# One scheduled graph of small tasks, with DMA transposes from block 3 on, for chunk-selected attention and a softplus MLP

## The chip, the cores and the metric

The kernel runs on one core of a Trainium2 chip. A core has a matmul engine (TensorE, PE in the profile), a vector engine (VectorE, DVE), an activation engine (ScalarE, ACT), a general engine (GpSimd, POOL) and a queue engine (SyncE, SP). Each works through its own program in order; they meet at semaphores. Sixteen DMA engines move data. SBUF is the on-chip memory, PSUM the eight banks into which TensorE writes. The metric is the device time of one execution in microseconds (us).

## What is computed

```python
def _attn_ref(q, k, v):                      # (4, 8, 768, 64) each
    k_min, k_max = np.min(k_chunks, axis=3), np.max(k_chunks, axis=3)   # chunks of 32 keys
    ub = np.sum(np.maximum(q * k_min, q * k_max), axis=-1)              # a bound per query and chunk
    ub = np.where(causal, ub, -1000000000.0)
    top_chunks = np.argsort(ub, axis=-1)[..., -top_k:]                  # top_k = 6 of 24 chunks
    scores = scale * np.matmul(q, k.transpose(0, 1, 3, 2))
    mask = sel & (pos[:, None] >= pos[None, :])                         # chosen chunks, causal
    attn = softmax(np.where(mask, scores, -1000000000.0))
    return np.matmul(attn, v)

def _moe_ref(x, w_in, w_out):                # x (3072, 512), w_in (512, 2048), w_out (2048, 512)
    h = x @ w_in
    g = np.maximum(h, 0.0) + np.log1p(np.exp(-np.abs(h)))               # softplus
    return g @ w_out
```

The heads of the attention output side by side (8 x 64 = 512) are the MLP's input. Inputs and outputs are float32; the kernel computes in bfloat16 with float32 sums.

## The kernel before

The work is cut into 12 blocks: 4 batches by 3 blocks of 256 queries. A block goes through three stages.

The preparation (`prep_block`, L163) transposes k and q on TensorE by the identity matrix (L175, L191) so that the head dimension lies on partitions, two heads a tile; `kT` goes to SBUF on ScalarE (L179), and VectorE takes maximum and minimum of each chunk (L181, L182). Positive and negative parts of q (L203, L204) times these give the bounds `ub` (L212, L213, 48 columns each). VectorE adds the causal mask, finds the eight largest (L224), and writes which chunks lie below the sixth (`mraw`, L226). This is transposed too (`mT`, L236) and put beside q into `qa` and `qt`, so that the score matmul itself, with one-hot rows `ohb` in `KA` and `KB`, pushes chunks that were not chosen far down.

The attention goes by head pair `p` and head `h`: scores (L263, L265), the exponential on ScalarE into `pt` (L267), the causal mask of the diagonal on GpSimd (L271), then `o_ps` from `pt` and v (L285), one over the sum (L291), the product (L293), a transpose (L304) and a copy into the MLP's input `x` (L305).

The MLP: `hp` from `w_in_sb` and `x` (L322), exponential (L324) and logarithm of one plus it (L326) on ScalarE, which is the softplus, then `y` from `g` and `w_out_sb` (L335), a copy (L340) and a store of 128 rows.

The order is written out by hand. `run_block` walks the score steps of one block; after each, `slot` advances one waiting step of `later` (L285 and on), some steps of `mlp_stream` by a rate, whatever `agenda` has for this slot (the preparation of the next block, in five pieces) and one load. The lines that set it:

```python
        credit[0] += rate
        while credit[0] >= 1.0:
            credit[0] -= 1.0
            if next(mlp, "end") == "wait":
                credit[0] = 0.0
        for g_ in agenda.pop(clock[0], []):
            next(g_, None)
        if loads and next(loads[0], "end") == "end":
            loads.popleft()
```

Blocks 0 to 2 are loaded as float32 from SyncE and ScalarE (L90) and cast on ScalarE (L103); the others are loaded and cast by DMAs issued on GpSimd (L108, L114), as are the weights (L149, L155). Four DMAs from SyncE fill the one-hot rows (L142, L143). PSUM is split into fixed pools: two banks for scores, one for `o_ps`, two for transposes and bounds, two for `hp`, one for `y`.

Of the kernel before, what the change touches and what calls it, by code (L numbers as in the profile page):

```python
# [15 lines left out]
ET = mybir.EngineType  # L16


@with_exitstack
def kernel(  # L20
# [10 lines left out]
    B, H, S, D = q.shape  # L31
    CH = 32
    NCH = S // CH
    TOPK = 6
    NQT = S // 128
    NP = H // 2
    scale = 1.0 / math.sqrt(D)
    NEG = -30000.0 / scale

    d_model, d_ff = moe_w_in.shape  # L40
    KDM = d_model // 128
    KFF = d_ff // 128
    QB = 256
    NT = QB // 128
    NBLK = S // QB
    NCB = QB // CH
    blocks = [(b, blk) for b in range(B) for blk in range(NBLK)]
    NB = len(blocks)

    ctx.enter_context(tc.manual_schedule(engines={ET.Pool, ET.SP}))  # L50
    nc.scalar.preload_act_table_set("natural_log_exp_and_others")

    PS = bass.MemoryType.PSUM
    singles = ctx.enter_context(tc.tile_pool(name="singles", bufs=1))
    f_pool = ctx.enter_context(tc.tile_pool(name="f", bufs=6))
    io_pool = ctx.enter_context(tc.tile_pool(name="io", bufs=3))
    qt_pool = ctx.enter_context(tc.tile_pool(name="qt", bufs=3))
    prep = ctx.enter_context(tc.tile_pool(name="prep", bufs=2))
    pt_pool = ctx.enter_context(tc.tile_pool(name="pt", bufs=3))
    st_pool = ctx.enter_context(tc.tile_pool(name="st", bufs=3))  # L60
    x_pool = ctx.enter_context(tc.tile_pool(name="x", bufs=4))
    g_pool = ctx.enter_context(tc.tile_pool(name="g", bufs=3))
    e_pool = ctx.enter_context(tc.tile_pool(name="e", bufs=3))
    mo_pool = ctx.enter_context(tc.tile_pool(name="mo", bufs=3))
    ps_s = ctx.enter_context(tc.tile_pool(name="ps_s", bufs=2, space=PS))
    ps_o = ctx.enter_context(tc.tile_pool(name="ps_o", bufs=1, space=PS))
    ps_t = ctx.enter_context(tc.tile_pool(name="ps_t", bufs=2, space=PS))
    ps_h = ctx.enter_context(tc.tile_pool(name="ps_h", bufs=2, space=PS))
    ps_y = ctx.enter_context(tc.tile_pool(name="ps_y", bufs=1, space=PS))

    V = [singles.tile([128, NQT, H, D + 1], BF16, name=f"v_{i}") for i in range(2)]
    KA = [singles.tile([128, NP, S], BF16, name=f"ka_{i}") for i in range(2)]
    KB = [singles.tile([128, NP, S], BF16, name=f"kb_{i}") for i in range(2)]
    BD = [singles.tile([128, NP, 2, 2, NCH], BF16, name=f"bd_{i}") for i in range(2)]
    Mraw = [singles.tile([128, NP, NT, 2, 32], BF16, name=f"mraw_{i}") for i in range(2)]
    w_in_sb = singles.tile([128, KDM, d_ff], BF16, name="w_in_sb")
    w_out_sb = singles.tile([128, KFF, d_model], BF16, name="w_out_sb")

    src = {"k": k, "q": q, "v": v}
    xfs, loaded = {}, {}  # L80

    def rows(nm, n, t):
        b, blk = blocks[n]
        r0 = blk * QB + t * 128
        return src[nm][b, :, r0:r0 + 128].rearrange("h s d -> s h d")

    def load_f32(nm, n, eng):
        xf = f_pool.tile([128, NT, H, D], F32, name="xf")
        for t in range(NT):
            eng[t].dma_start(out=xf[:, t], in_=rows(nm, n, t))  # L90
        xfs[nm, n] = xf

    def v_dst(n, t):
        b, blk = blocks[n]
        return V[b % 2][:, blk * NT + t, :, 0:D]

    def cast_f32(nm, n):
        xf = xfs.pop((nm, n))
        if nm != "v":
            loaded[nm, n] = io_pool.tile([128, NT, H, D], BF16, name=nm + "_sb")  # L100
        for t in range(NT):
            dst = v_dst(n, t) if nm == "v" else loaded[nm, n][:, t]
            nc.scalar.copy(dst, xf[:, t])  # L103

    def load_cast(nm, n):
        if nm == "v":
            for t in range(NT):
                nc.gpsimd.dma_start(out=v_dst(n, t), in_=rows(nm, n, t))  # L108
                yield
        else:  # L110
            xb = io_pool.tile([128, NT, H, D], BF16, name=nm + "_sb")
            loaded[nm, n] = xb
            for t in range(NT):
                nc.gpsimd.dma_start(out=xb[:, t], in_=rows(nm, n, t))  # L114
                yield

    for nm in "kqv":
        load_f32(nm, 0, (nc.sync, nc.scalar))

    ident = singles.tile([128, 128], BF16)  # L120
    make_identity(nc, ident)
    ohb = singles.tile([32, S], BF16, name="ohb")
    nc.vector.memset(ohb, NEG)
    cmask = singles.tile([128, NQT, NCH], F32, name="cmask")
    nc.vector.memset(cmask, 0.0)
    nc.gpsimd.affine_select(out=ohb, in_=ohb, compare_op=ALU.is_ge, fill=0.0,
                            base=0, channel_multiplier=-CH, pattern=[[1, S]])
    nc.gpsimd.affine_select(out=ohb, in_=ohb, compare_op=ALU.is_ge, fill=0.0,
                            base=CH - 1, channel_multiplier=CH, pattern=[[-1, S]])
    nc.gpsimd.affine_select(out=ohb, in_=ohb, compare_op=ALU.not_equal, fill=-1.0,  # L130
                            base=-NCH, channel_multiplier=1, pattern=[[0, S]])
    nc.gpsimd.affine_select(out=cmask, in_=cmask, compare_op=ALU.is_ge, fill=-1.0e30,
                            base=0, channel_multiplier=1, pattern=[[128, NQT], [-CH, NCH]])

    for i in range(2):
        nc.vector.memset(Mraw[i], 0.0)

    def consts(i):
        nc.vector.memset(BD[i], 0.0)
        nc.vector.memset(KB[i][0:32], 0.0)  # L140
        nc.vector.memset(V[i][:, :, :, D:D + 1], 1.0)
        nc.sync.dma_start(out=KA[i][64:96], in_=ohb.unsqueeze(1).to_broadcast([32, NP, S]))  # L142
        nc.sync.dma_start(out=KB[i][32:64], in_=ohb.unsqueeze(1).to_broadcast([32, NP, S]))  # L143

    def load_w_in():
        for half in range(2):
            fs = slice(half * d_ff // 2, (half + 1) * d_ff // 2)
            for kt in range(KDM):
                nc.gpsimd.dma_start(out=w_in_sb[:, kt, fs],  # L149
                                    in_=moe_w_in[kt * 128:(kt + 1) * 128, fs])  # L150
                yield

    def load_w_out():
        for c4 in range(4):
            nc.gpsimd.dma_start(  # L155
                out=w_out_sb[:, c4 * 4:(c4 + 1) * 4, :],
                in_=moe_w_out[c4 * 512:(c4 + 1) * 512, :].rearrange(
                    "(kt ki) f -> ki kt f", ki=128))
            yield

    Q = {}

    def prep_block(n):  # L163
        b, blk = blocks[n]
# [81 lines left out]
        yield  # L246

    later = deque()
    clock = [0]
    X = {}  # L250

    def score_step(n, p):
# [234 lines left out]
```

The softmax here doesn't subtract the row's maximum and nothing guards it: scores larger than these inputs give would overflow.

## Time and profile before

| | |
|---|---|
| time, median of 2 runs | 316.94 us (316.83 to 317.06) |
| span of the profiled execution | 314.1 us |
| busy: PE, ACT, DVE, POOL | 270.5, 224.2, 174.4, 99.0 us |
| chain that ended last, by engine | PE 57%, DVE 26%, ACT 12% |
| PE matmuls of L322, L335 (busy) | 103.5, 90.7 us |
| score exponentials (L267), MLP exponentials (L324), logarithms (L326) | 103.9, 58.4, 51.8 us |
| DMA engines' share of q0 (issued on GpSimd) | 43.9% of the span |

The profile is of one execution. A group of instructions is given by its line, its engine, the tiles written and read and a count; behind the bar stand its busy time and the mean of one. Matmuls are pipelined: their durations overlap, and the gap between two starts says more than a duration. A timeline row is the start, the time covered, and what ran; "x8" means that eight equal instructions are merged; brackets hold the idle time before it and what ended that. In the row by slices each digit is the busy share of a fortieth of the span, in tenths.

### The profile page before, as it was taken

How to read it: one execution, taken by the hardware profiler on the slowest of the kernel's cores; microseconds unless marked ns; L12 is line 12 of the kernel's file. 1: busy time of each engine (PE TensorE's matmuls, PEld its weight loads, DVE VectorE, ACT ScalarE, POOL GpSimd, SP SyncE). 2: the span in 40 equal slices, each digit the busy share in tenths (PEclk: the TensorE clock that was granted, in tenths of full speed). 3: DMA queues.
4: the chain of work that ended last, by engine and by line, in shares of the span. 5: the costliest groups of instructions: out<-in, count | busy, mean ns of one | idle time of the engine just before them, and what ended most of it. 6: DMA issues, size and time to landing. Idle time of an engine off the chain costs nothing.

```text
span 314.1 us, 6878 instructions
## 1 busy us (share of the span) xinstructions
PE 270.5 (86%) x2748; PEld 198.6 (63%) x2784; DVE 174.4 (56%) x550; ACT 224.2 (71%) x379; POOL 99.0 (32%) x172
## 2 busy tenths in 40 slices
PE   1335879989899799899999799899999999999983
PEld 0223657667658667677658577677568777776651
DVE  5818582592965964935946946836748732112100
ACT  4578789968837858788628868888539769983550
POOL 4024375622723613514624414424421211111000
PEclk9999959999999999999999999999999999999999
DMA  9999899993933906904913905907900000001101
GB/s 165 200 216 216 147 158 189 92 71 45 80 73 52 83 11 60 101 2 57 90 59 53 83 35 33 102 3 76 94 33 35 3 33 35 2 33 35 67 17 52
DMA packets 82208, 23.51 MB, mean 75 GB/s; under 512 B 75520, under 2 KB 78080, under 8 KB 82176
## 3 DMA queue, kind: packets, MB, share of 16 engines
q0 software_dynamic: 59424, 11.28, 43.9%
q1 hardware_dynamic: 19632, 11.01, 14.3%
q10 hardware_dynamic: 3120, 0.79, 1.4%
q8 instruction: 21, 0.34, 0.4%
q14 instruction: 11, 0.09, 0.1%
HBM read 27.26 MB, written 6.29 MB: 107 GB/s over the span
## 4 chain that ended last, share of the span: by engine, by line
PE 57%; DVE 26%; ACT 12%; issue 2%; DMA 1%; ACTq 0%; DVEq 0%
PE y L335 21%; PE hp L322 17%; PE o_ps L285 5%; PE s_ps L263 4%; DVE kx L181 4%; ACT kt L179 4%; DVE kx L182 4%; PE s_ps L265 3%; PE mT L236 3%; ACT pt L267 2%; DVE qneg L204 2%; ACT e_sb L324 2%; DVE qpos L203 2%; DVE qt L200 2%; DMA xf<-in_k_dram 1%
## 5 line engine op out<-in xcount | busy, mean ns | idle before, releaser
L267 ACT ACTIVATE pt<-s_ps 128x512 bf16<-128x512 f32 (+1 forms) x192 | 103.9, 556 | 36.7 <-PE s_ps L265 29.9
L322 PE MATMUL hp<-x,w_in_sb 128*128 128x256 bf16 x768 | 103.5, 273 | 3.2 <-ACT e_sb L324 1.8
L271 POOL TENSOR_SCALAR_AFFINE_SELECT pt<-pt 128x256 bf16<-128x256 bf16 x96 | 40.9, 426 | 185.5 <-ACT pt L267 185.1
L335 PE MATMUL y<-w_out_sb,g 128*128 128x512 bf16 x348 | 90.7, 379 | 3.6 <-DVE y_sb L340 1.7
L322 PEld LDWEIGHTS <-w_in_sb 128*128 128x128 bf16 x768 | 71.4, 98 | 12.9 <-issue 4.1
L324 ACT ACTIVATE e_sb<-hp 128x512 f32<-128x512 f32 x96 | 58.4, 611 | 27.7 <-PE hp L322 27.4
L335 PEld LDWEIGHTS <-g 128*128 128x128 bf16 x384 | 34.2, 97 | 28.6 <-issue 2.8
L326 ACT ACTIVATE g<-e_sb 128x1024 bf16<-128x1024 f32 x48 | 51.8, 1078 | 0.3
L285 PEld LDWEIGHTS <-pt 128*128 128x128 bf16 x672 | 32.9, 99 | 11.1 <-issue 4.3
L340 DVE COPY y_sb<-y 128x512 f32<-128x512 f32 x24 | 16.5, 687 | 39.7 <-PE y L335 39.5
L291 DVE RECIPROCAL rec<-o_ps 128x4 f32<-128x4 f32 x48 | 8.5, 177 | 38.1 <-PE o_ps L285 37.9
L305 DVE COPY x<-oT 128x256 bf16<-128x256 bf16 x48 | 13.9, 289 | 25.1 <-PE oT L304 24.8
L285 PE MATMUL o_ps<-v_106,pt 128*128 128x65 bf16 x336 | 20.7, 199 | 2.2 <-DVE o_sb L293 1.9
L181 DVE TENSOR_REDUCE kx<-kt 128x32 bf16<-128x1024 bf16 x12 | 14.6, 1219 | 13.0 <-ACT kt L179 13.0
L293 DVE TENSOR_TENSOR o_sb<-o_ps,rec 128x256 bf16<-128x256 f32 x48 | 20.2, 422 | 1.3
L285 PE MATMUL o_ps<-v_107,pt 128*128 128x65 bf16 x336 | 18.4, 193 | 1.7 <-DVE o_sb L293 1.5
L304 PE MATMUL oT<-ident,o_sb 128*128 128x128 bf16 x96 | 13.7, 225 | 4.3 <-DVE o_sb L293 4.3
L114 POOL DMA_DIRECT2D k_sb<-in_k_dram x18 | 16.1, 892 | 0.8 <-issue 0.5
L114 POOL DMA_DIRECT2D q_sb<-in_q_dram x18 | 16.2, 902 | 0.4 <-issue 0.3
L175 PE MATMUL kT<-ident,k_sb 128*128 128x128 bf16 x96 | 8.8, 241 | 8.1 <-ACT k_sb L103 7.6
L263 PE MATMUL s_ps<-qt,kb_110 128*128 128x256 bf16 x48 | 14.0, 293 | 1.6 <-ACT pt L267 0.9
L263 PE MATMUL s_ps<-qa,ka_108 96*128 96x256 bf16 x48 | 14.2, 296 | 0.8 <-DVE qa L241 0.8
(111 smaller groups left out, 365.2 us busy)
## 6 DMA issues: line engine op xcount, KB each, us to landing
out_dram<-y_sb SPq DMA_DIRECT2D x24, 256.0 KB, 2.0
k_sb<-in_k_dram POOLq DMA_DIRECT2D x18, 128.0 KB, 3.8
q_sb<-in_q_dram POOLq DMA_DIRECT2D x18, 128.0 KB, 4.3
w_in_sb<-in_moe_w_in_dram POOLq DMA_DIRECT2D x8, 256.0 KB, 6.9
w_out_sb<-in_moe_w_out_dram POOLq DMA_DIRECT2D x4, 512.0 KB, 9.5
v_107<-in_v_dram POOLq DMA_DIRECT2D x12, 128.0 KB, 5.3
xf<-in_k_dram SPq DMA_DIRECT2D x5, 256.0 KB, 5.1
xf<-in_q_dram SPq DMA_DIRECT2D x5, 256.0 KB, 5.8
```

The lines of the kernel that those rows point to most:

```text
L114: nc.gpsimd.dma_start(out=xb[:, t], in_=rows(nm, n, t))
L181: nc.vector.tensor_reduce(kx[:, :, 0], kT4, axis=AX.X, op=ALU.max)
L263: nc.tensor.matmul(s_ps[:, 0:QB], kk[0:nr, p, j * 128:(j + 1) * 128], qq[0:nr, p, :], start=True, stop=True)
L267: nc.scalar.activation(pt[:, h, j:j + 2].rearrange("k j c -> k (j c)")[:, 0:w], s_ps[:, 0:w], ACT.Exp, scale=scale)
L271: nc.gpsimd.affine_select(out=diag, in_=diag, compare_op=ALU.is_ge, fill=0.0, base=0, channel_multiplier=-1, pattern=[[0, 2], [1, 128]])
L285: nc.tensor.matmul(o_ps[:, u, h], pt[:, h, j, c0:c0 + 128], V[b % 2][:, j, 2 * p + h, :], start=(j == 0), stop=(j == t0 + u))
L293: nc.vector.tensor_tensor(o_sb, o_ps[:, :, :, 0:D], rec.to_broadcast([128, NT, 2, D]), op=ALU.mult)
L322: nc.tensor.matmul(hp[:, fi], w_in_sb[:, dt, ft * 128:(ft + 1) * 128], X[n][:, dt], start=(dt == 0), stop=(dt == KDM - 1))
L324: nc.scalar.activation(e_sb[:, f2 * 2:f2 * 2 + 2], hp, ACT.Exp)
L326: nc.scalar.activation(g[:, f4 * 4:(f4 + 1) * 4], e_sb, ACT.Ln, bias=1.0)
L335: nc.tensor.matmul(y, g[:, f, u * 128:(u + 1) * 128], w_out_sb[:, f, :], start=(f == 0), stop=(f == KFF - 1))
L340: nc.vector.tensor_copy(y_sb, y)
```

## The change

The program is no longer written out as nested generators. `build` describes the whole kernel as small tasks, each with an engine, a modelled duration, a priority, and the keys that it reads and writes; `Graph.schedule` then places them at build time: for each engine it takes, whenever the engine is free in the model, the ready task of lowest priority number whose buffers are to be had. Buffers, PSUM banks among them, come from pools and are given out by the same model. The order that comes out is the program. On the chip every engine runs its part in that order, held by semaphores. Its purpose is to let every engine find work that is ready, and to fit the PSUM banks to what is going on.

Beside the order, these things change:

- From block 3 on, k, q, the selection mask and the attention output are transposed by DMA (`dma_start_transpose`, on SyncE), not on TensorE.
- In blocks 0 to 2 k and q are transposed on TensorE as float32, straight from the loaded tiles (by `identf`); ScalarE copies k into `ka` and `kb` from PSUM and q into `qb`. v is cast on GpSimd.
- One-hot rows are copied on GpSimd and no longer by DMA.
- PSUM is one pool of eight banks with a cap for each use. `pt` has six half-size buffers.
- Bounds are computed only for the chunks up to the block (`ncc` columns in place of 24 per head).
- The weights' loads have no place in a hand-written order: they wait in the graph for the cast of v of block 2, and follow by priority.

```diff
-    ctx.enter_context(tc.manual_schedule(engines={ET.Pool, ET.SP}))
+    ctx.enter_context(tc.manual_schedule(engines={ET.Pool, ET.SP, ET.Activation, ET.DVE, ET.PE}))
...
+LAT = {"PE": 0.23, "ACT": 0.20, "DVE": 0.15, "POOL": 0.15, "SP": 0.0}
+PSUM_CAP = {"s": 3, "h": 3, "y": 2, "o": 2, "t": 3}
...
+    g = Graph({"ps": 8, "xf": 8, "kq": 4, "kt": 2, "qab": 6, "qpn": 4, "kx": 2, "ub": 2, "mr": 2,
+               "mt": 2, "pt": 6, "st": 4, "oall": 2, "osb": 3, "x": 5, "g": 3, "e": 3, "yo": 2}, PSUM_CAP)
...
+                add("POOL", 0.55, lambda half=half, kt=kt: ld_win(half, kt), 14 + half * 2 + kt * 0.1,
+                    w=[("w_in", half, kt)], dma=1.38, lat=0.7, name="ldw_in", after=WGATE)
+        for c4 in range(4):
+            add("POOL", 0.75, lambda c4=c4: ld_wout(c4), 20 + c4, w=[("w_out", c4)], dma=3.1, lat=0.7, name="ldw_out",
+                after=WGATE)
...
+                add("POOL", 0.9, ld, max(base, 24 + n) + i, w=w, dma=2.1, lat=0.7, name=f"ld{nm}{n}")
...
+                add("PE", 0.44, tr, pr, r=[xk, "identf"], w=[kT], name=f"kT{n}")
...
+            def tr(ks=ks, kt=kt):
+                SP.dma_start_transpose(T(kt), T(ks).rearrange("s t c -> s (t c)"))
+            add("SP", 1.3, tr, pr, r=[(ks, 0), (ks, 1)], w=[kt], dma=0.9, lat=1.5, name=f"kTd{n}")
...
+                SP.dma_start_transpose(T(qb), T(qs).rearrange("s t c -> s (t c)"))
...
+                SP.dma_start_transpose(T(mt), T(mr).rearrange("s t p c -> s (t p c)"))
+            add("SP", 1.3, tr, pr + 3, r=[(mr, 0), (mr, 1)], w=[mt], dma=0.9, lat=1.5, name=f"mTd{n}")
...
+                add("ACT", 0.375 if last else 0.482, ex, pr_s + 0.2, r=[sp], w=[(pt, j)], name=f"ex{n}")
...
+                    add("POOL", 0.38, cm, pr_s, r=[(pt, j)], w=[(pt, j)], name=f"cm{n}")
...
+        elif p == NP - 1:
+            add("SP", 1.3, lambda: SP.dma_start_transpose(T(x), T(osb).rearrange("s t p h d -> s (t p h d)")), pr + 1.5,
+                r=[(osb, p_) for p_ in range(NP)], w=[(x, p_) for p_ in range(NP)], dma=0.9, lat=1.5, name=f"oTd{n}")
...
+                    add("PE", 0.438, hm, pr + 0.01 * fi, r=[(x, p) for p in range(NP)] + [("w_in", half, k) for k in range(KDM)],
+                        w=[(hp, fi)], name=f"h{n}")
...
+    order = graph.schedule()
...
+    for t in order:
+        t.fn()
```

In the program that comes out of it, GpSimd's part runs as follows up to the masks of block 3. A load issued on GpSimd carries a wait for the load eight places before it; this was so in the kernel before as well.

```
constants, one-hot rows; casts of v, block 0
k block 3 (2 loads); one-hot rows of the second set; 8 masks of block 0; casts of v, block 1
q block 3 (2), k block 4 (2), v block 3 (2)
6 masks of block 1, between them q block 4 (2) and casts of v, block 2
v block 4 (1), w_in (8)
the last 2 masks of block 1
w_out (4), v block 4 (1), k block 5 (2), q block 5 (2)
mask, 2 loads, mask, load, mask, load, 2 masks, load, mask      (block 2's first three head pairs)
2 masks (block 3's first head pair), load, 2 masks (block 2's last pair)
```

TensorE's part has its first MLP matmul behind the first pair of block 3 in this list.

## The prediction

> **What bounds the kernel now.** I read the page by slices first, then busy times by stretch, then the order of time on TensorE and GpSimd, then the waits. The slices:
>
> ```profile
> PE   1335879989899799899999799899999999999983
> DMA  9999899993933906904913905907900000001101
> ```
>
> Until about 57 us the DMA engines are full and TensorE fills slowly; afterwards it is the other way round. The busy times by stretch (PE, PEld, DVE, ACT, POOL, clock, DMA share, GB/s), all work, then the first MLP matmuls (L322) alone:
>
> ```profile
> 0.00:60.00 60.00, 35.95 (x353) 27.11 (x355) 33.40 (x117) 45.78 (x74) 23.90 (x46) 0.94 1.23 180
> 60.00:295.00 235.00, 221.74 (x2318) 163.63 (x2350) 138.93 (x431) 170.81 (x297) 75.05 (x126) 1.00 0.48 51
> ...
> 0.00:60.00 60.00, 9.59 (x64) 6.22 (x64) 0.94 1.23 180
> ```
>
> At 60 us only 64 of 768 matmuls of L322 are done. From there PE is busy 221.7 of 235 us, ACT 171, DVE 139: TensorE is the bound. Since busy time overstates it, I price its work by start-to-start gaps from the order of time:
>
> ```profile
> 122.08 0.61 PE L175 MATMUL kT<-ident,k_sb 128*128 128x128 bf16 x8
> 122.53 0.28 PE L263 MATMUL s_ps<-qa,ka_109 96*128 96x256 bf16 x1
> 122.64 0.27 PE L265 MATMUL s_ps<-qa,ka_109 96*128 96x256 bf16 x1
> ...
> 134.37 0.53 PE L285 MATMUL o_ps<-v_107,pt 128*128 128x65 bf16 x12
> 134.73 1.03 PE L322 MATMUL hp<-x,w_in_sb 128*128 128x256 bf16 x8
> ...
> 295.21 3.66 PE L322 MATMUL hp<-x,w_in_sb 128*128 128x256 bf16 x32
> ...
> 305.10 3.61 PE L335 MATMUL y<-w_out_sb,g 128*128 128x512 bf16 x16 [0.78 <-DVE y_sb L340]
> ```
>
> So a transpose costs 0.45/8 = 0.056 us, a score matmul 0.11 (128 columns 0.055, from 123.84 to 123.90), one of L285 0.36/12 = 0.030, of L322 (3.66-0.27)/31 = 0.109, of L335 (3.61-0.38)/15 = 0.215, and a bound matmul (L212, L213) 0.40/16 = 0.025. After 60 us there remain 704 of L322 (77.0 us), 380 of L335 (81.7), 249 score matmuls of 256 columns (27.4) and 79 of 128 (4.3), 592 of L285 (17.8), 282 transposes (15.8) and 144 bound matmuls (3.6): 227.6 us. They take from 60 to 308.7, that is 248.7 us, a density of 91.5%. Behind the last matmul lie 5.4 us of span (y copy 0.69, store, end), and the time is 2.8 us above the span.
>
> On GpSimd the order of time shows masks and loads taking turns, and the waits up to 60 us name ACT, never a DMA:
>
> ```profile
> 35.81 0.40 POOL L271 TENSOR_SCALAR_AFFINE_SELECT pt<-pt 128x256 bf16<-128x256 bf16 x1 [0.52 <-ACT pt L267]
> 36.16 0.55 POOL L149 DMA_DIRECT2D w_in_sb<-in_moe_w_in_dram  x1
> 38.00 0.40 POOL L271 TENSOR_SCALAR_AFFINE_SELECT pt<-pt 128x256 bf16<-128x256 bf16 x1 [1.29 <-ACT pt L267]
> 38.45 1.53 POOL L155 DMA_DIRECT2D w_out_sb<-in_moe_w_out_dram  x2
> ```
>
> ```profile
> POOL pt L271 <- ACT pt L267: 32.3, 10, 15.1
> ```
>
> **What the Trainium skill says.** "TensorE: Matmul & The Clock Gate", section "Back-to-back issue gap", gives N/2.4 + 2.5 ns for a warm matmul: 109 and 216 ns for 256 and 512 columns, and the trace has 109 and 215. "DMA: Bandwidth & Descriptors", section "Issuing engines are not separate DMA queues", says that DMAs from all issuing engines share the same 16 engines; the trace agrees (a share of 1.23 up to 60 us, first-block loads of v landing only after 7.5 to 8.9 us). For the added transposes the pages disagree. "Advanced Engine Details and Errata", section "X-Bar Transpose (TRN2)", calls them as fast as ordinary DMAs. "DMA: Bandwidth & Descriptors", section "Why a DMA increments its semaphore by 16 and not by 1", has in its table on the later chip's faster path 262,144 sequencer cycles for 8,192 tiles on earlier generations, so 32 a tile. No run here shows one yet.
>
> **The change, part by part.**
>
> *Transposes leave TensorE.* For blocks 3 to 11 the transposes of k, q, the selection mask and the attention output go to 36 DMA transposes of 256 KB on SyncE. PE loses 9 x (8+8+8+8) x 0.056 = 16.1 us, nearly all on the bound. With them go the ACT copies of kT (12 x 1.02 us) and the DVE copies out of PSUM of qT and oT; neither engine was the bound, so I count nothing. The cost of one DMA transpose: the planner in the change has 1.3 us of SyncE, 0.9 of transfer and 1.5 of latency. Low end: that. High end: if that tile is 256 bytes (as the same page's section "SDMA does more than copy" has it), one transfer has 1,024 tiles and 32,768 cycles, an estimated 27 us at the 1.2 GHz that "Trainium Kernel Development and Optimization", section "NeuronCore Architecture", gives SyncE. I take the low one, since the planner's other prices agree with this trace (0.438 for four matmuls of L322, here 4 x 0.109; 0.482 for an exponential of 512, here 0.47 between two). Then they hide: each is due 14 us before its block's scores, SyncE has about 4 x 1.3 + 2 x 0.6 = 6.4 us of issue in a block of some 20 us. Behind a waiting transpose on SyncE stand output stores and the next block's transposes; behind them DVE's reductions.
>
> *The ramp.* Blocks 0 to 2 transpose f32 straight from the loads: 18 casts of 0.62 us go from ACT (11.2 us, L103), 2 x 24 transposes become f32 ones. Behind the first k tile (landed at 4.8 us) this saves about 1 us of chain. The MLP's first matmul now stands in PE's program behind three of block 2's four head pairs and the first of block 3: 152 of 672 L285-type matmuls and 102 of 384 score matmuls. In the kernel before, 80 and 56 were done at 60 us. Work is moved forward, into time in which PE was waiting for weights.
>
> *A new wait on GpSimd.* Every load issued there waits for the load eight places before it. In the new program the eight loads of w_in stand in one row (with 11 k, q, v loads before them), then two masks, then four of w_out and five more loads, then the masks of block 2, each between loads. A load that waits now holds masks behind it; for them wait the L285-type matmuls, for these PE in order, MLP included. So the MLP starts when w_out and about 13 k, q, v loads have landed. Before, the engines were full until 57 us with 18 f32 loads, 4 one-hot copies, 12 weight loads and 6 k, q, v loads. Seven more loads at about 1.4 us (six issued over 5.4 us land within some 10 us, less 2 of latency) add 10; the one-hot copies, now made on GpSimd, give back 4 (0.79 MB at 200 GB/s) to 10. That is 57 to 63 us; I take 58, since the k, q, v loads start early. Low end 48: w_in was in before at 36.2 + 7 us, plus a few loads.
>
> *The rest.* PE's work from there, at the same prices: 768 of L322's kind 84.0, 384 of L335's 82.6, 213 and 69 score matmuls 23.4 + 3.8, 520 of L285's 15.6, 112 bound matmuls 2.8, together 212.3 us. Beside it ACT has some 150 us to do (142 score exponentials at about 0.43, 96 of the MLP at 0.47, 48 logarithms at 0.94, as gaps in the order of time), and DVE had 139 of 235 us before, with fewer PSUM copies now: neither ends the stretch.
>
> *The order and the PSUM pool.* One pool of eight banks with caps replaces fixed pairs (y and o had one bank each), and every instruction is placed by modelled costs. Before, 248.7 - 227.6 = 21.1 us were lost. The named part of it (oT behind o_sb 4.3, o_ps behind o_sb 3.0, y behind y_sb 1.7) goes; in-order queues with loads that land at other times than modelled bring some back. I take half: 10 us, a density of 95.5%.
>
> Sum: 58 + 222.3 + 5.4 + 2.8 = 288.5, so 288 us.
>
> **The rivals.**
>
> *A, forecast (0.55):* 288 us.
>
> *B, GpSimd's row of waits hides (0.16):* masks get through between landings and the MLP starts at 48 us, at 98% density (the MLP-only stretch from 280 to 300 shows PE at 19.75 of 20): 48 + 216.6 + 8.2 = 273. For it: the DMA queue is fed earlier. Against it: nine waits in a row in the program.
>
> *C, the order drifts (0.19):* the start is at 63 and density stays at 91.5%, since a static order meets late loads: 63 + 232 + 8.2 = 303. For it: five in-order queues, all tied to each other. Against it: the prices agree with the trace.
>
> *D, the DMA transposes become the bound (0.10):* SyncE must issue 36 of them and 24 stores. The old time would be reached at 36t + 14.4 = 251, t = 6.6 us each. At 27 us it is 58 + 983, over 1,000 us, far slower than before.
>
> **How the numbers follow.** The predicted time is A's. The range, 268 to 306, runs from below B to above C and leaves D out. Faster 0.88: A, B and C but for a little of C; same 0.03; slower 0.09, from D.
>
> **What would show it.** The PE row of the slices should rise to 9 near 58 us with no MLP before it, and stay there until attention is through. GpSimd's waits should now name DMA before 60 us, ahead of masks: if they don't, the third step is wrong. DMA transposes should land within 4 us and no DVE reduction wait on them for long; a SyncE issue of several microseconds each would make D true. PE from its first MLP matmul to its last should take about 222 us; over 230 means drift. The gap from last matmul to end should still be about 5 us.

## The result, and the profile after

The changed kernel takes 299.5 us (298.97 and 300.07) against 316.9 us before: a ratio of 0.946, 95% interval 0.940 to 0.953. It is faster, as forecast, and 11.5 us slower than forecast (288 us, range 268 to 306). A kernel's time, here and below, is the median of its runs without those that took over 1.5% longer than its fastest.

The rows of TensorE, its granted clock and the DMA engines, in 40 slices of 7.4 us, of the changed kernel:

```profile
PE   2637652705999999999999999999999999999994
PEclk9999995565699999999999999999999999999999
DMA  8995999999997158999999984699544211020001
```

TensorE's row reaches 9 with the eleventh slice, which begins at 74 us, and keeps it up to the last slice. The digits before it, down to 0 in the ninth slice (59 to 67 us), are the poor ones; the row of before had no such hole. The DMA row stands at 7 or more in most slices up to 178 us, with a gap from about 97 to 111. Busy time by stretch (columns: PE, PEld, DVE, ACT, POOL, granted clock, DMA share, GB/s), all instructions:

```profile
40.00:60.00 20.00, 9.06 (x100) 6.50 (x98) 16.27 (x63) 6.80 (x16) 13.57 (x21) 0.66 1.18 161
60.00:80.00 20.00, 10.14 (x121) 8.52 (x122) 7.10 (x31) 6.93 (x16) 10.22 (x16) 0.57 1.75 172
80.00:100.00 20.00, 19.89 (x204) 15.73 (x203) 5.44 (x24) 16.94 (x33) 9.87 (x17) 1.00 0.87 68
...
80.00:293.43 213.43, 211.62 (x2041) 155.69 (x2068) 92.64 (x342) 164.69 (x288) 57.76 (x103) 1.00 0.68 86
```

The first MLP matmul (L629) starts at 79.95 us and the last matmul ends at 293.4. Between them lie 213.4 us, of which TensorE is busy 211.6. Put in the forecast's own terms:

| term | forecast | measured | difference |
|---|---|---|---|
| start of the MLP | 58 | 80.0 | +22.0 |
| from there to the last matmul | 222.3 | 213.4 | -8.9 |
| last matmul to the end of the span | 5.4 | 3.9 | -1.5 |
| time above the span | 2.8 | 1.7 | -1.1 |
| sum (profiled execution) | 288.5 | 299.0 | +10.5 |

So the small miss in the total hides two larger ones of opposite sign: that the total came so near is in part luck. What TensorE waited for up to 95 us (line, releaser, us in total, times, longest):

```profile
PE ps L572 <- POOL pt L562: 10.7, 3, 6.2
PE ps L458 <- DVE qpn L444: 7.2, 5, 3.6
PE ps L601 <- DVE osb L593: 5.8, 4, 3.1
PE ps L369 <- DMA xf<-in_k_dram: 4.9, 1, 4.9
PE ps L488 <- DVE mr L478: 4.9, 4, 2.2
PE ps L542 <- DVE qab L493: 4.3, 3, 1.8
```

The longest wait is the forecast's: L572 for the masks of block 2. But VectorE's lines together are 22.2 us. In GpSimd's order of time the forecast wait is plain to see:

```profile
57.65 0.87 POOL L342 DMA_DIRECT2D kq<-in_q_dram  x1 [0.51 <-DMA w_in_sb<-in_moe_w_in_dram]
61.43 0.87 POOL L342 DMA_DIRECT2D kq<-in_q_dram  x1 [2.92 <-DMA w_out_sb<-in_moe_w_out_dram]
62.31 0.42 POOL L562 TENSOR_SCALAR_AFFINE_SELECT pt<-pt 128x256 bf16<-128x256 bf16 x1
64.80 1.14 POOL L340 DMA_DIRECT2D v<-in_v_dram  x1 [2.07 <-DMA w_out_sb<-in_moe_w_out_dram]
68.13 0.88 POOL L340 DMA_DIRECT2D v<-in_v_dram  x1 [2.19 <-DMA w_out_sb<-in_moe_w_out_dram]
69.02 0.42 POOL L562 TENSOR_SCALAR_AFFINE_SELECT pt<-pt 128x256 bf16<-128x256 bf16 x1
```

Each of these k, q or v loads waits for the part of w_in or w_out issued eight loads before it, and a mask of block 2 stands behind them: the ones at 62.3 and 69.0 us end the waits of 3.6 and 6.2 us. The planner's own model, which knows nothing of this wait, had block 2's masks at 45.7 to 56.4 us and the first MLP matmul at 56.0. VectorE's order of time shows something that the forecast had not thought of:

```profile
51.43 1.35 SPq L504 DMA_TRANSPOSE mt<-mr  x1
```

```profile
63.80 0.42 DVE L506 COPY qab<-mt 32x1024 bf16<-32x1024 bf16 x1 [7.21 <-DMA mt<-mr]
```

Block 3's mask transpose was issued at 51.4 us and its copy could start at 63.8: 12.4 us, while the weights were coming in, and VectorE stood still for 7.2 us of them. The issues and landings up to 80 us (number, median us from issue to landing), where over the whole run the median is 4.5 us for kt, 4.7 for qab, 4.3 for mt and 2.9 for x:

```profile
kt<-kq SPq DMA_TRANSPOSE x2, 4.3
qab<-kq SPq DMA_TRANSPOSE x2, 11.2
mt<-mr SPq DMA_TRANSPOSE x1, 12.4
```

The 11.2 is the middle of two very different ones. The three transposes issued from 25 to 37 us, before the first load of a weight, landed after 3.5 to 5.1 us; the two issued at 51.4 (mt) and 52.9 us (qab), with the weights in flight, after 12.4 and 17.5. They are no exception among the transfers of that time: the k, q and v loads that GpSimd issued from 53 to 62 us took 14 to 18 us.

My theory after this: the start is late because block 2 waits in GpSimd's row of loads. The rivals: VectorE, busy 51.2 of the first 60 us, bounds the ramp; the DMA engines do, through the weights' arrival or through the first transposes. And a second question: whose is the gain, the scheduler's or the transposes'?

### The profile page after: what moved, and what is told of

Its sections match the earlier page's. It is cut to its first block, busy times and chain, and to the rows that moved or that the text cites. A ratio compares the mean times of both kernels' runs of the same rounds, so it can differ in the third digit from the quotient of the medians.

```text
span 297.3 us, 6510 instructions
## 1 busy us (share of the span) xinstructions
PE 252.8 (85%) x2465; PEld 188.0 (63%) x2496; DVE 151.6 (51%) x553; ACT 198.4 (67%) x355; POOL 113.5 (38%) x184
## 3 DMA queue, kind: packets, MB, share of 16 engines
q1 hardware_dynamic: 57072, 19.67, 35.5%
## 4 chain that ended last, share of the span: by engine, by line
PE 69%; DMA 12%; DVE 11%; issue 2%; POOL 2%; ACT 1%; SPq 1%; DVEq 0%; ACTq 0%
PE ps L629 27%; PE ps L651 25%; DMA w_out_sb<-in_moe_w_out_dram 6%; PE ps L542 6%; PE ps L572 6%; DMA w_in_sb<-in_moe_w_in_dram 3%; PE ps L547 3%; DVE kx L379 2%; DMA qab<-kq 2%; PE ps L545 1%; DMA xf<-in_k_dram 1%; DVE ub L470 1%; DVE mr L476 1%; DVE qpn L444 1%; DVE bd L413 1%
## 5 line engine op out<-in xcount | busy, mean ns | idle before, releaser
L556 ACT ACTIVATE pt<-ps 128x512 bf16<-128x512 f32 (+1 forms) x192 | 92.1, 574 | 35.0 <-PE ps L547 26.4
L629 PE MATMUL ps<-x,w_in_sb 128*128 128x256 bf16 x768 | 106.3, 272 | 0.1
L651 PE MATMUL ps<-w_out_sb,g 128*128 128x512 bf16 x353 | 99.2, 379 | 1.2
L629 PEld LDWEIGHTS <-w_in_sb 128*128 128x128 bf16 x768 | 73.2, 98 | 26.9
L636 ACT ACTIVATE e<-ps 128x512 f32<-128x512 f32 x96 | 57.3, 620 | 37.9 <-PE ps L629 37.4
L640 ACT ACTIVATE g<-e 128x1024 bf16<-128x1024 f32 x48 | 51.6, 1076 | 0.9
L656 DVE COPY yo<-ps 128x512 f32<-128x512 f32 x24 | 16.5, 691 | 56.0 <-PE ps L651 55.2
L651 PEld LDWEIGHTS <-g 128*128 128x128 bf16 x384 | 35.5, 98 | 14.9 <-ACT g L640 0.2
L572 PE MATMUL ps<-v,pt 128*128 128x65 bf16 x672 | 31.3, 200 | 10.8 <-POOL pt L562 10.7
L572 PEld LDWEIGHTS <-pt 128*128 128x128 bf16 x672 | 28.5, 102 | 14.7 <-POOL pt L562 11.1
L542 PE MATMUL ps<-qab,ka 96*128 96x256 bf16 x96 | 27.1, 297 | 4.4 <-DVE qab L493 4.3
L542 PE MATMUL ps<-qab,kb 128*128 128x256 bf16 x96 | 26.9, 291 | 0.2
L342 POOL DMA_DIRECT2D kq<-in_q_dram x18 | 16.3, 907 | 12.8 <-DMA qab<-kq 9.3
```

What stands on the lines that cost most here:

```text
L342: PO.dma_start(out=T(b_)[:, t].rearrange("s (h d) -> s h d", h=H), in_=rows(nm, n, t))
L542: PE.matmul(T(sp)[:, 0:QB].rearrange("k (t s) -> k t s", t=NT), kk[r0:r1, j, p], qv[r0:r1, :, p], start=True, stop=True)
L556: AC.activation(T(pt)[:, j:j + 2].rearrange("k j c -> k (j c)")[:, 0:w], T(sp)[:, 0:w], ACT.Exp, scale=SCALE)
L572: PE.matmul(o[:, u, h], T(pts[h])[:, j, c0:c0 + 128], T("v", i)[:, j, 2 * p + h, :], start=(j == 0), stop=(j == t0 + u))
L629: PE.matmul(o, T("w_in")[:, dt, ft * 128:(ft + 1) * 128], xv[:, :, dt], start=(dt == 0), stop=(dt == KDM - 1))
L636: AC.activation(T(e)[:, f2 * 2:f2 * 2 + 2].rearrange("f a s -> f (a s)"), T(hp), ACT.Exp)
```

## The experiments

All kernels compute the whole reference. Each kernel that changes the graph is planned anew, so beside its edit its order differs somewhat. "Start" is the first MLP matmul; "share" is TensorE's busy time between it and the last matmul.

| kernel | time, us | ratio to before, 95% interval | start, us | share |
|---|---|---|---|---|
| kernel before | 316.9 | | 35.7 | |
| changed kernel | 299.5 | 0.940 to 0.953 | 80.0 | 99% |
| one-hot rows by DMA | 296.7 | 0.934 to 0.940 | 75.8 | 99% |
| VectorE's relief | 297.6 | 0.937 to 0.943 | 77.1 | 99% or more |
| planner knows eight loads | 297.2 | 0.934 to 0.943 | 67.1 | 95% |
| blocks 3, 4 on TensorE | 292.5 | 0.918 to 0.930 | 64.9 | 99% |
| eight loads + relief | 290.5 | 0.916 to 0.924 | 59.2 | 97% |
| eight loads + relief + blocks 3, 4 on TensorE | 281.4 | 0.885 to 0.892 | 55.9 | 98% |
| all transposes on TensorE | 309.4 | 0.976 to 0.985 | 62.3 | 98% |
| old kernel with DMA transposes | 309.1 | 0.971 to 0.983 | 35.2 | |

### Whose gain: the transposes or the scheduler

*All transposes back on TensorE, same scheduler.* For blocks 3 to 11 the four DMA transposes become 32 on TensorE, with copies out of PSUM (k's shown; q, mask and output in the same way):

```diff
-            def tr(ks=ks, kt=kt):
-                SP.dma_start_transpose(T(kt), T(ks).rearrange("s t c -> s (t c)"))
-            add("SP", 1.3, tr, pr, ...)
...
+                        PE.transpose(o[:, c:c + 128], T(ks)[:, t, p * 128:(p + 1) * 128], T("ident"))
...
+            add("PE", 0.45, tr, pr, r=[(ks, 0), (ks, 1), "ident"], w=[kps], name=f"kT{n}")
...
+            add("ACT", 0.95, kc, pr, r=[kps], w=[kt], name=f"kc{n}")
```

> The changed kernel with its four DMA transposes per block done on TensorE again (32 transposes and the copies out of PSUM for each of the 9 later blocks; k's copy on ScalarE, q's and the masks' on VectorE), everything planned anew by the same scheduler. It undoes the DMA half of the change and keeps the scheduling half. Theory: TensorE has no more than a per cent of idle time from its first MLP matmul on, so that the 288 transposes add their 16.1 us in full: 313 to 318 us, that is, all of the measured gain comes from the transposes, and what the scheduler gained in density it lost in its ramp. Rival (the gain is the scheduler's, the transposes fit into gaps): 299 to 305 us.

Measured: 309.4 us, between the two. The row from its start to its last matmul:

```profile
62.30:303.17 240.87, 236.28 (x2406) 174.57 (x2402) 119.82 (x420) 177.17 (x305) 66.32 (x115) 0.98 0.46 52
```

TensorE is as dense as expected (98%), and the stretch is 27 us longer than the changed kernel's, but it begins 18 us earlier, at 62.3. So with this scheduler the DMA transposes are worth 309.4 - 299.5 = 9.9 us, not 16: they save TensorE its time and give part of it back in the ramp. The rest of the change, which is the scheduler with its PSUM pool, the ramp in f32 and the shorter bounds, is worth 316.7 - 309.4 = 7.3 us; its parts were not run apart.

*DMA transposes alone, in the old kernel.* Its slots and queues stay; from block 3 on, k and q are transposed by DMA four slots ahead of their use, and the output at the end of its block. The masks' tile is padded, and two pools shrink by a buffer to make room:

```diff
+        nc.sync.dma_start_transpose(kt, k_sb.rearrange("s t h d -> s (t h d)"))
+        nc.sync.dma_start_transpose(qb, q_sb.rearrange("s t h d -> s (t h d)"))
+        yield
...
+        nc.sync.dma_start_transpose(mt, mpad.rearrange("s p t c -> s (p t c)"))
...
+            nc.sync.dma_start_transpose(xd, OALL.pop(n).rearrange("s t p h d -> s (t p h d)"))
+            agenda.setdefault(clock[0] + 4, []).append(landed())
```

> The kernel before, with its hand-written slots and queues, and from block 3 on the four transposes by DMA from SyncE, issued four slots ahead; the masks' tile is padded to 128 columns for it, and two pools shrink by a buffer. It does the DMA half of the change alone. If TensorE's work is what the old kernel waits for, its time falls by the 16.1 us of the transposes and by nothing else: 299 to 304 us. Rival (the old order's waits, 21 us from 60 us on, take up what TensorE gives back): 308 to 317 us.

Measured: 309.1 us (307.7 and 310.5; two further runs took 312.8 and 315.2), the rival's side. TensorE's waits from 90 us on:

```profile
PE hp L424 <- DMA x<-oall: 6.4, 5, 2.8
PE y L438 <- DVE y_sb L443: 4.5, 3, 2.0
PE o_ps L370 <- DVE oall L385: 1.9, 4, 0.6
```

The MLP now waits for the transposed attention output (L424 for x), and for VectorE. A fixed order has a fixed place for the consumer; where the transpose comes later than that, TensorE pays. In the old order the transposes are worth 316.7 - 309.1 = 7.6 us, with the scheduler 9.9, in neither the 16.1 of TensorE's work. The two figures lie too close, for a kernel whose times scatter so, to say that the order makes a difference here. What differs is where the rest is lost: in the old order in these waits, while the changed kernel's list of waits from 90 us on is empty and its loss is in the ramp.

### Why the start is late: GpSimd's row of loads

*The planner knows of eight loads.*

```diff
+        flying = 0
...
         def fits(t):
+            if t.eng == "POOL" and t.dma is not None and flying >= 8:
+                return False
...
                 elif what == "landed":
+                    if x.eng == "POOL":
+                        flying -= 1
...
+                    if t.eng == "POOL":
+                        flying += 1
                     post(now + 1.1, "queue", t)
```

> The planner alone is changed: it learns that GpSimd has no more than eight loads in flight, so it spreads the sixteen loads from w_in on over the time in which they can really start, and puts block 2's masks between them instead of behind them. Data, engines, transfers and buffers stay. Theory (block 2's masks stand behind GpSimd's waiting loads, and TensorE, in order, behind the masks): the first MLP matmul comes at about 60 to 65 us instead of 80, the 6.25 and 3.62 us waits of L572 for pt are gone, and the time falls by most of that, to 281 to 287 us. Rival 1 (the weights' arrival ends the ramp whatever the order is): first MLP matmul within 3 us of 80, time 297 to 300. Rival 2 (VectorE is full in the ramp and is what holds block 2): first MLP matmul at about 75, time about 294.

Measured: 297.2 us, start 67.1. The wait is gone as foretold: up to 95 us GpSimd now waits only for exponentials (POOL pt L569 <- ACT pt L563), and L579 for masks 1.0 us in all. The time fell by only 2.3 us. TensorE's waits up to 95 us tell why:

```profile
PE ps L549 <- DVE qab L513: 7.6, 1, 7.6
PE ps L495 <- DVE mr L485: 6.4, 4, 2.3
PE ps L465 <- DVE qpn L451: 6.1, 4, 2.8
...
PE ps L608 <- DVE osb L600: 4.4, 5, 2.0
```

VectorE's three lines (L495, L465, L608: 16.9 us) are what they were in the changed kernel (17.9). In the masks' place stands one new wait, 7.6 us at L549 for the mask rows of qab. It comes behind the start, and is most of what the stretch from the start to the last matmul grew by (224.3 us in place of 213.4). VectorE's own order of time has its cause:

```profile
80.40 0.42 DVE L513 COPY qab<-mt 32x1024 bf16<-32x1024 bf16 x1 [8.05 <-DMA mt<-mr]
```

SyncE issued this kernel's first two mask transposes, and between them the second of q, as follows:

```profile
52.76 1.23 SPq L511 DMA_TRANSPOSE mt<-mr  x1
54.16 1.26 SPq L443 DMA_TRANSPOSE qab<-kq  x1
68.58 1.33 SPq L511 DMA_TRANSPOSE mt<-mr  x1
```

The last, which the wait is for, took 11.8 us to land, behind four parts of w_out issued from 63.2 to 67.3 us. The first two took 4.1 and 3.5 us: they fell into the time from 46.3 to 56.1 us in which GpSimd issued no load. Besides, the reverse of the old wait came up on GpSimd:

```profile
44.10 2.16 POOL L318 DMA_DIRECT2D w_in_sb<-in_moe_w_in_dram  x4
55.77 0.40 POOL L569 TENSOR_SCALAR_AFFINE_SELECT pt<-pt 128x256 bf16<-128x256 bf16 x1 [9.51 <-ACT pt L563]
56.12 0.55 POOL L318 DMA_DIRECT2D w_in_sb<-in_moe_w_in_dram  x1
```

The planner puts a mask of block 2 between two loads of w_in; block 2 is late on the chip, so the load waits for the mask. On one queue in order, whichever stands in front holds the other when the model is off.

*The weights' loads not held back for block 2's v*, alone and with the planner's knowledge:

```diff
-                    WGATE.append(c)
+                    pass
```

> One line of the graph is changed: the loads of the weights no longer wait for the casts of block 2's v, so that the planner issues w_in right behind block 0's casts; the planner still knows nothing of the eight loads in flight. Theory (GpSimd's order): the MLP of block 0 can start before block 2 is attended, at 35 to 45 us, and the time falls to 275 to 288, though the masks of block 0 now stand behind the first load of w_out, which has to wait for the first loads of w_in. Rival 1 (the DMA engines are what is full in the ramp): the 8 MB of weights only push back the inputs of blocks 1 and 2, TensorE starves later instead of earlier, and the time stays within 3 us of 299.5.

> Both edits together: the planner knows of the eight loads in flight, and the weights' loads do not wait for block 2's v. Theory (GpSimd's order holds the ramp): the first MLP matmul at 30 to 40 us, no mask behind a waiting load before 55 us, time 264 to 275 us, which would be under both kernels. Rival 1 (DMA full): within 3 us of the kernel with the planner's knowledge alone. Rival 2 (VectorE full in the ramp): the MLP starts early but block 2 and block 3 come no earlier, time 283 to 290.

Measured: 302.6 us (300.2 to 304.1) and start 45.0 alone; with the planner's knowledge start 35.3 and four times spread from 283.6 to 292.8 us, so no ratio is given. The MLP starts 35 to 45 us earlier than in the changed kernel, and yet the time alone is 3 us worse, near its rival's "within 3 us of 299.5". With the planner's knowledge all four times are better than the changed kernel's and none comes near the 264 to 275 us of the theory. In both the share falls to 93%. The first of TensorE's waits from 20 us on, in the kernel with this edit alone:

```profile
PE ps L369 <- DMA xf<-in_k_dram: 13.7, 2, 9.1
```

The inputs of the first blocks now come behind the weights, and attention is late. An early start alone is no gain.

### Why the start is late: VectorE

*The second one-hot rows by DMA.*

```diff
-            PO.tensor_copy(dst, src.to_broadcast([32, NQT, NP, 128]))
+            if i == 0:
+                PO.tensor_copy(dst, src.to_broadcast([32, NQT, NP, 128]))
+            else:
+                for p in range(NP):
+                    SP.dma_start(out=dst[:, :, p], in_=T("ohb").rearrange("c (j s) -> c j s", s=128))
```

> The two copies of the one-hot rows of the second key tiles (2.74 us each on GpSimd at 13.6 and 16.4 us) are written by four small DMA each from SyncE, at the same place in the order; nothing else is moved. Theory of contention (GpSimd's copy slows VectorE): the small copies of L476 that took 1.46 and 2.78 us beside them take 0.2 to 0.3 us, and VectorE's ramp is some 4 us shorter. Does the time follow? If VectorE bounds the ramp (rival 2): 295 to 296 us. If GpSimd's waiting loads bound it (the theory): 298.5 to 300 us, first MLP matmul within 1.5 us of 80. If there is no such contention, L476 still shows copies of over 1 us.

Measured: 296.7 us, 2.8 us less, start 75.8. VectorE in the changed kernel, then GpSimd in the same time:

```profile
14.93 1.46 DVE L476 TENSOR_TENSOR mr<-ub 128x64 bf16<-128x64 f32 x1
16.32 0.17 DVE L478 CAST mr<-ub 128x8 bf16<-128x8 f32 x1
16.39 2.78 DVE L476 TENSOR_TENSOR mr<-ub 128x64 bf16<-128x64 f32 x1
```

```profile
13.58 2.74 POOL L276 COPY ka<-ohb 32x3072 bf16<-32x3072 bf16 x1
16.36 2.74 POOL L276 COPY kb<-ohb 32x3072 bf16<-32x3072 bf16 x1
```

And VectorE with the rows by DMA:

```profile
14.93 0.20 DVE L480 TENSOR_TENSOR mr<-ub 128x64 bf16<-128x64 f32 x1
15.06 0.17 DVE L482 CAST mr<-ub 128x8 bf16<-128x8 f32 x1
15.13 0.21 DVE L480 TENSOR_TENSOR mr<-ub 128x64 bf16<-128x64 f32 x1
```

The 0.2 us instruction ended each time just after a GpSimd copy did (16.32 and 19.10). The Trainium skill, "GPSIMD Engine Reference", section "1. Specifications", says that GpSimd shares its SBUF interfaces with VectorE, with contention where a VectorE instruction has two SBUF inputs. L476 compares two SBUF operands; the trace agrees. Instructions with an operand in PSUM kept their time beside GpSimd's copies: L379 took 0.69 us beside the first two copies and 0.68 behind the last, and two of L464 at 13.55 us took 0.47 us, 0.48 with the rows by DMA. What returned is 3.8 us of VectorE and 2.8 us of time, more than the theory of GpSimd alone allowed (298.5 or more). GpSimd is freed of 5.5 us by the same edit, but it was not short of time there: behind the two copies it stood idle for 4.7 us until the first exponential.

*VectorE's relief*: the one-hot rows by DMA, and besides the ramp's mask copies and output copies to ScalarE, and one clearing earlier:

```diff
-                    DV.tensor_copy(T(qa)[64:96, t * NP:(t + 1) * NP], o[64:96])
+                    AC.copy(T(qa)[64:96, t * NP:(t + 1) * NP], o[64:96])
...
-                DV.tensor_copy(T(x).rearrange("d (u p) s -> d u p s", u=NT)[:, :, p], o)
+                AC.copy(T(x).rearrange("d (u p) s -> d u p s", u=NT)[:, :, p], o)
...
-        add("DVE", 1.35, lambda i=i: DV.memset(T("kb", i)[0:32], 0.0), -7 + i * 30, ...
+        add("DVE", 1.35, lambda i=i: DV.memset(T("kb", i)[0:32], 0.0), -7 + i, ...
```

> VectorE alone is relieved in the first three blocks: the one-hot rows of the second key tiles by DMA as before, the twelve mask copies out of PSUM (0.42 us each) and the twelve copies of the output's transposes (0.28 us each) to ScalarE, which is idle for half of that time, and the second clearing of kb (1.34 us) ahead of the first input. The planner still does not know of the eight loads in flight. If VectorE bounds the ramp, block 2's scores come some 8 us earlier than in the kernel with the one-hot rows alone moved, first MLP matmul at 68 to 70 us, time 288 to 291 us. If GpSimd's waiting loads bound it, the masks still wait for w_out's landing and the MLP starts at 74 to 76 us: 295 to 297 us.

Measured: 297.6 us, start 77.1, no better than the one-hot rows alone. VectorE's busy time in 20 to 40 us fell from 19.25 to 12.74 us, and the freed time went into the other wait, in TensorE's list up to 95 us:

```profile
PE ps L576 <- POOL pt L566: 15.3, 5, 12.2
PE ps L462 <- DVE qpn L448: 9.7, 5, 5.4
```

The masks are now 15.3 us of waiting (10.7 before): GpSimd's row bounds this kernel, the expectation's second case (295 to 297 us, start 74 to 76), though it lies just above both figures.

*Both*, the planner's knowledge and the relief (the two diffs above):

> VectorE's relief and the planner's knowledge of the eight loads in flight together. Each alone has been seen to leave the other's wait in place. If the two causes are in series (either of them alone holds block 2), together they give more than the sum of 2.3 us (planner's knowledge) and the relief's own gain: first MLP matmul at 58 to 62 us, time 281 to 286 us. If they only add up: 288 to 293 us. If the weights' arrival is a third bound: TensorE waits for w_in at its first MLP matmuls, 290 us or more.

Measured: 290.5 us, start 59.2. Alone the two gave 2.3 and 1.9 us, together 9.0: they stand in series, each hiding behind the other. The start was as foretold and the time not (281 to 286 us foretold). TensorE's share is 97%; the largest single wait after the start, in its order of time, and what VectorE does before it:

```profile
73.41 0.27 PE L553 MATMUL ps<-qab,ka 96*128 96x256 bf16 x1 [3.15 <-DVE oall L604]
```

```profile
71.72 0.42 DVE L517 COPY qab<-mt 32x1024 bf16<-32x1024 bf16 x1 [6.04 <-DMA mt<-mr]
72.15 0.53 DVE L519 COPY qab<-mt 32x1024 bf16<-32x1024 bf16 x1
72.71 0.18 DVE L592 RECIPROCAL st<-ps 128x4 f32<-128x4 f32 x1
72.93 0.42 DVE L604 TENSOR_TENSOR oall<-ps,st 128x256 bf16<-128x256 f32 x1
```

The transpose of block 3's mask was issued at 61.64 us and took until 71.7. VectorE, in order, stood at the copy that needs it, and behind that copy stands L604, which TensorE waits for.

### Why the start is late: the first DMA transposes

*Blocks 3 and 4 on TensorE*, in the changed kernel and in the one with both edits. The same code as for all transposes, under `if n < 5`:

```diff
-        if ramp:
+        if n < 5:
             for t in range(NT):
                 mT = ps("t")
```

> VectorE's relief and the planner's knowledge of eight loads as in the run before, and blocks 3 and 4 transposed on TensorE as the first three are; DMA transposes from block 5 on. In the run before, the mask transpose of block 3 was issued at 61.6 us and its copies could start at 71.7, because it shared the DMA engines with w_out and the next inputs; TensorE stood still for 3.15 us at 73 us. Theory (DMA transposes are cheap only when the DMA engines are not full): this wait goes, and the 64 transposes that come back to TensorE (3.6 us) go partly into its gaps before 75 us: 285 to 289 us. Rival (the DMA latency is hidden by the planner's order anyway): the 3.6 us are added: 293 to 295 us.

> The changed kernel with one edit: blocks 3 and 4 are transposed on TensorE, DMA transposes begin with block 5. VectorE's ramp, the one-hot rows on GpSimd and the planner's ignorance of eight loads stay. It takes the third suspected cause alone, as two runs before took the other two (2.3 and 2.0 us each). In the changed kernel the first transposes of q and of the mask, issued between 50 and 60 us beside the weights, landed after 11 to 12 us. If these transposes alone hold the ramp: first MLP matmul at 62 to 66 us as in the kernel with all transposes on TensorE, 287 to 291 us. If the three causes stand in series, so that each alone leaves the next one in place: start at 72 to 78 us, 296 to 300 us. If the DMA latency plays no part with the old order: 80 us, and the 64 transposes back on TensorE make it 300 to 303 us.

Measured with both edits: 281.4 us, 9.1 less than without, under both kernels and better than the expectation's best, though TensorE has 64 transposes (3.6 us) more to do. Its waits from 30 us to the end:

```profile
PE ps L584 <- ACT qab L535: 1.9, 2, 1.4
PE ps L614 <- ACT qab L539: 1.1, 1, 1.1
```

The start is 55.9, the share 98.3%. TensorE's idle time before the start went from 59.2 - 38.2 = 21.0 us to 55.9 - 39.8 = 16.1, after it from 7.5 to 3.7. In both kernels GpSimd waits for no DMA up to 95 us, so GpSimd's row has no part in the 9.1 us; how much of them is the transposes' landing (the 3.15 us wait at 73 us is gone), how much their traffic, the new order or the copies of blocks 3 and 4 that the relief now puts on ScalarE, was not separated.

With nothing else changed (the second expectation; the landings that it puts at 11 to 12 us were 12.4 and 17.5): 292.5 us, 7.0 less, start 64.9; the start lies in the first case of the expectation, the time between the first two. Here the reading is less clean. The planner also placed four of block 2's masks ahead of loads that wait for w_out (at 54.2 and 55.9 us, where the changed kernel has none from 47 to 62), and TensorE's wait for masks fell from 10.7 to 4.2 us. So most of the 7.0 us may be order and not landing. That the first DMA transposes cost time is shown by the waits behind their landing (7.6 us in the kernel with the planner's knowledge, 3.15 in the one with both edits); how much of the 7.0 and 9.1 us is theirs is open.

### Two more that don't pay

*The three edits of GpSimd's order and VectorE's relief together* (relief, eight loads, weights not held back):

> The three edits together: VectorE's relief, the planner's knowledge of the eight loads, and no wait of the weights' loads for block 2's v. The weights come in first and the inputs of blocks 1 and 2 later. Theory (after the two causes are gone only the DMA engines' total is left in the first 100 us): first MLP matmul at 25 to 35 us, TensorE half idle until 60 us because the inputs come later, 280 to 286 us, some 5 us under the same kernel with the weights' loads held back. Rival (the order of the transfers doesn't matter because their sum ends at the same time): within 2 us of 290.5 us.

Measured: 288.8 us (287.3 to 290.0): the rival's case. The profiled execution took 293.3 us, so its account is a hint only: start 34.0, share 93%; with the weights first, the inputs come later (GpSimd's casts of v, L524, wait 14.2 us for them up to 95 us), and TensorE, dense from 60 to 80 us, has 7.6 us of idle time from 80 to 140.

*The planner's load costs scaled by 0.7*, on the kernel with both edits (`dma=1.38` to 0.97, 3.1 to 2.17, 2.1 to 1.47):

> Like the kernel with the relief and the knowledge of eight loads, and the planner's costs for GpSimd's loads are scaled by 0.7, so that it believes them to land sooner and issues the later ones sooner. Nothing else. In that kernel, the loads of blocks 5 and 6 stood behind masks that waited up to 4.9 us for an exponential, and TensorE then waited 1.45 us at 106 and 1.39 us at 117 us for what depends on them. Theory (loads behind masks cost the density that the early start brings): TensorE's busy share from the first MLP matmul on rises from 96.7% to 98% or more, 284 to 288 us. Rival (the DMA engines themselves are the limit, and loads that are issued sooner hold the masks again): 290 us or more, with GpSimd waiting for DMA ahead of masks as in the changed kernel.

Measured: 290.9 us (289.5 and 292.3; two further runs took 293.9 and 294.6), against 290.5 without the edit: the rival's case. The profiled execution is the one of 294.6 us, with start 42.5 and share 93.5%; two of TensorE's waits in it from 30 us on:

```profile
PE ps L553 <- DVE qab L517: 9.9, 3, 4.9
PE ps L583 <- POOL pt L573: 4.7, 3, 3.4
```

Masks are waited for again (L583), and so is qab, which needs the mask transposes (L517); GpSimd waits 5.9 us for w_in up to 95 us, as the rival said. Cheaper loads in the planner's model, by this one factor, brought nothing.

## Why the prediction was right, and where it was wrong

*What bounds the kernel.* Right. In the changed kernel TensorE bounds all that comes after the start, with DMA full until then.

*Transposes leave TensorE.* The low end of the price was right for the issue (most took 1.23 to 1.6 us of SyncE, planner 1.3; the longest, at 52.9 us, 6.64) and far from the high one of 27 us. The transfer was mis-sized: SyncE's queue took 12.5% of 307.7 us with all transposes on TensorE and takes 35.5% of 297.3, 67.1 us more for 36 transposes, so 1.9 us of all 16 engines' packet time each and not 0.9. The step's "then they hide" failed for two of the first: 12.4 and 17.5 us to landing beside the weights. Of the 16.1 us, 9.9 reached the time. "DMA: Bandwidth & Descriptors", section "Queues, rings and completion order", has each engine alternate between the queues that have work, packet by packet; a transpose of 1,056 packets ((57,072 - 19,056)/36, the smaller count being that of the kernel with all transposes on TensorE) landing late beside a queue full of loads fits that. No run here shows the alternation itself.

*The ramp.* The step counted TensorE's and ScalarE's side (a chain 1 us shorter) and not VectorE's. VectorE is busy 51.2 of the first 60 us, where it was busy 33.4 before: it now has all the mask copies out of PSUM (12 of 0.42 us), the waits behind GpSimd's copies (3.8 us), and the preparation of later blocks moved forward. The f32 reductions out of PSUM (8.0 us for three blocks, 7.3 before) are not the difference. The f32 transposes were given no price either; eight of L369 take 1.94 us, but TensorE was not what was short. The planner's knowledge alone brought the start to 67.1, with the relief to 59.2: this is a part of the 22 us.

*A new wait on GpSimd.* The mechanism was right, with each load, mask and releaser as described, but the date was not: 58 us was taken, 80.0 measured. The step summed transfers as if the weights were on their way as early as in the old kernel, where GpSimd issued w_in from 20.1 to 36.2 us; here w_in could be issued only from 41.9 us on, behind block 2's casts, and w_out at 47.8 to 52.3, each part of w_out then landing after 13 to 19 us. It also took the wait for the only bound of the start; without it the start was still 67.1, and the time 2.3 us less.

*The order and the PSUM pool.* Mis-sized to the other side: 95.5% was assumed, and the 212.3 us of work took 213.4. With all transposes on TensorE and a start of 62.3 TensorE is still busy for 98% of the stretch, where the old kernel had 94% from 60 us to its last matmul. In the kernel whose start was the forecast one (59.2), the stretch took 225.6 us and the time was 290.5, close to the forecast's 222.3 and 288.5; that kernel's loss was the late transposes and loads, and with blocks 3 and 4 on TensorE it rose to 98%. The forecast was thus near a kernel that was not the one built.

*The rivals.* B (the waits hide, start 48) and D (transposes on SyncE become the bound) are out. C came nearest in time (303) with a wrong reason: its late start was there, its low density not.

## What to carry to other kernels

A planner that models engines and DMA makes a static order, and an order is only as good as the waits it knows: list every queue's hidden limits (loads in flight, a shared port, the landing of a transfer beside a full queue) before trusting its start date. Moving work from TensorE to DMA pays where the DMA engines have room: here the transposes of blocks 3 and 4, beside the weights, were better left on TensorE. When waits stand in series, removing one can show almost nothing in the time (2.3 and 1.9 us here, 9.0 for both): look in the trace whether its wait is gone and which one came in its place.

## What was not expected of the hardware

- A VectorE instruction with two SBUF inputs stood still until a GpSimd copy had ended: 1.46 and 2.78 us in place of 0.2.
- The granted clock of TensorE was 0.66 in 40 to 60 us and 0.57 in 60 to 80 of the changed kernel, where TensorE is half idle, and 1.00 after. Where it is low, score matmuls of 256 columns started 0.21 us apart in the kernel with the planner's knowledge (54.36 and 54.57 us), in place of 0.11. What lowers it was not tried.
- A DMA transpose of a 128x1024 tile took 2.9 to 4.7 us to land in the median, and 12.4 and 17.5 us beside the weights. Its issue took SyncE 1.3 us as a rule; the one at 52.9 us, beside the weights, held SyncE for 6.64 us.
